# Head of a fused convolution and feed-forward kernel: dense conv of block 2 moved ahead of the second stage of block 0, a third of a weight copied by GpSimd, loads of x5 to x8 issued earlier, three matmuls on zeros fewer

## The chip, the cores and the metric

One core of one Trainium2 chip runs the whole program. The metric is the device time of one execution in microseconds (us). Eight executions of the kernel before have a median of 483.81 us, the lowest 480.97 and the highest 485.81.

## What is computed

```python
# x: (8, 4160, 192), weight: (8, 7), w1, w2, w3: (192, 768), w_out: (768, 192), all float32
w = softmax(weight, axis=-1)                  # one 7-tap filter for each of 8 heads
x_pad = zeros of 6 rows ahead of each sequence, then x
y[b, s, head h, :] = sum over k of w[h, k] * x_pad[b, s + k, head h, :]   # 24 channels a head
y = y.reshape(33280, 192)
h = max(max(y @ w1, y @ w2), y @ w3)
out = h @ w_out                               # (33280, 192) float32
```

## The kernel before, in words

**Blocks.** The 33280 tokens are cut into 65 blocks of 512. The maximum of three products is taken as a difference: with c = y w3, it is c + max(relu(y (w1 - w3)), y (w2 - w3)). So `make_wd` forms the two differences (tile wd, the upper 64 partitions for w1, the lower ones for w2), and the added c is folded into the second product through M = w3 w_out, which `make_m` computes once (tile m). For that, w3 is cast (`cast_w3`), transposed on TensorE (`transpose_w3`) and multiplied by w_out (tile wo). `copy_w3` copies w3 from partitions 0 to 63 to partitions 64 to 127 (tile w3s), in three parts of 256 columns, since the w2 half of `make_wd` needs it there: part 0 serves differences 0 and 1, part 1 serves 2 and 3, part 2 serves 4 and 5.

**Stages of a block t.** `load_x(t)` issues the DMA of its rows from SyncE's queue (SP). `cast_x(t)` casts them to float16 on GpSimd (POOL). `conv(t)` multiplies by a band matrix on TensorE (tile G), `evac` takes the result to SBUF (ys), `repack(t)` moves six pieces by DMA from the SP and POOL queues into the layout of the next product (yd), and `double(t)` copies yd to the other 64 partitions by DMA. Blocks 0 to 3 go another way, "dense": `cast_dense` writes two zero-padded copies (xz), `conv_dense` makes the convolution already in the right layout with 120 smaller matmuls (tile D), and the other half of yd comes from `cross` (three VectorE copies, blocks 0 and 1) or `cross_dma` (two DMAs on SP, blocks 2 and 3). Then `l1(t, j)`, for j of 0 to 5, makes 128 of the 768 hidden columns: three matmuls for lp and three for lq, interleaved, ScalarE's relu of lp (r, L376) and VectorE's maximum of r and lq (h, L377). `st2(t, u, 6)` is the second stage, in six parts: products of h by wo and of yd by m (po), ScalarE's copy a (L425), VectorE's sum o (L426). `store(t, ...)` writes the block.

**What sets the order.** Each engine works through its instructions in the order in which the kernel text issues them; the order is written by hand, and only waits on semaphores tie the engines. Lines 453 to 506 are the head: blocks 0 and 1, with the making of the weights woven in. From line 512 a loop over t = 2 to 64 issues l1(t, 0), two convolutions every second block, and then st2(t - 1, j) after each l1(t, j). `keep_warm(n)` (L213) issues n matmuls on a tile of zeros.

**Buffers that bind.** lp and lq have two PSUM buffers each, so l1 number k waits until r, or h, of number k - 2 is done. G, D, po and the zero matmuls share four others. Raw rows xf: blocks 0, 3 and 5 use one buffer, 1, 2 and 4 another, and from block 6 on there are four; so load_x(5) waits for cast_dense(3), and load_x(6) to load_x(9) wait for nothing. x16 (the cast rows) has four buffers.

**Lines to find.** The head's order is L453 to L506: cross(0) L459, make_wd(1, 2) L460, the zero matmuls L466, L468 and L474, copy_w3 part 2 on ScalarE L477, make_wd(4, 6) L479, cast_dense(2) L491, st2(0, 0) L492, conv_dense(2) L496, cross_dma(2) L497, load_x(5) and load_x(6) L500 and L501. In the loop, repack(4), load_x(7) and the casts of x5 and x6 are L531 to L534, and load_x(8) is L537.

Of the kernel before, what the change touches and what calls it, by code (L numbers as in the profile page):

```python
# [27 lines left out]
def kernel(  # L28
# [12 lines left out]
    nc = tc.nc  # L41
# [6 lines left out]
    NJ = DFF // P  # L48
# [105 lines left out]
    NC, NSLOT, CYC = D // HALF, D // 32, 96  # L154
# [54 lines left out]
    def keep_warm(n, pool=psw, tag="w"):  # L209

        ps = pool.tile([P, NBLK], FP32, tag=tag, name="idle")
        for _ in range(n):
            nc.tensor.matmul(ps[:], lhsT=idle[:, 0:P], rhs=idle[:], start=True, stop=True)  # L213
# [36 lines left out]
    def make_wd(j0, j1):  # L250
        f = slice(P * j0, P * j1)
        nc.vector.tensor_sub(out=wd[:, :, f], in0=ws[:, :, f], in1=w3s[:, :, f])  # L252

    def copy_w3(copy, part):
        f = slice(PW * part, PW * (part + 1))
        copy(out=w3s[HALF:P, :, f], in_=w3s[0:HALF, :, f])

    def cast_w3(part):
        f = slice(PW * part, PW * (part + 1))
        nc.gpsimd.tensor_copy(out=w3h[:, :, f], in_=w3s[0:HALF, :, f])  # L260

    def transpose_w3(g):
        ps = psw.tile([P, 2, D], FP32, tag="w", name=f"pt{g}")
        for k in range(2):
            js = slice(P * (2 * g + k), P * (2 * g + k + 1))
            for c in range(NC):
                nc.tensor.matmul(ps[:, k, HALF * c:HALF * (c + 1)], lhsT=w3h[:, c, js],
                                 rhs=ident16[0:HALF, 0:HALF], start=True, stop=True)
        nc.scalar.copy(out=w3t[:, 2 * g:2 * g + 2, :], in_=ps[:])
# [54 lines left out]
            else:  # L324
                copies[2](out=yd[0:HALF, 2, :], in_=ps[0:HALF, :])

    def cross(t):

        yd = dense[t]
        for c in range(NC):  # L330
            a, b = (slice(HALF, P), slice(0, HALF))[::-1 if c == 1 else 1]
            nc.vector.tensor_copy(out=yd[a, c, :], in_=yd[b, c, :])  # L332

    def cross_dma(t):
        yd = dense[t]
        nc.sync.dma_start(out=yd[HALF:P, 0:NC:2, :], in_=yd[0:HALF, 0:NC:2, :])
        nc.sync.dma_start(out=yd[0:HALF, 1, :], in_=yd[HALF:P, 1, :])
# [25 lines left out]
    def l1(t, j):  # L363


        N, y = blkN[t], dense[t]
        ps = [pool.tile([P, NBLK], FP32, tag=tag, name=f"l{tag}_{t}_{j}")
              for pool, tag in ((psp, "p"), (psq, "q"))]
        for c in range(NC):
            for i in range(2):  # L370
                row = slice(HALF * i, HALF * (i + 1))
                nc.tensor.matmul(ps[i][:, 0:N], lhsT=wd[row, c, P * j:P * (j + 1)],  # L372
                                 rhs=y[row, c, 0:N],
                                 start=(c == 0), stop=(c == NC - 1))
        r = rp.tile([P, NBLK], FP16, tag="r", name=f"r_{t}_{j}")
        nc.scalar.activation(out=r[:, 0:N], in_=ps[0][:, 0:N], func=AF.Relu)  # L376
        nc.vector.tensor_max(out=hs[t][:, j, 0:N], in0=r[:, 0:N], in1=ps[1][:, 0:N])  # L377

    def st2(t, u, NU):

        if t < 0:
            return
        hT, y = hs[t], dense[t]
        if u == 0:
            todo = [[], []]
            for s in range(4):
                tok = slice(P * s, P * (s + 1))
                for i in range(2):  # L390
                    row = slice(HALF * i, HALF * (i + 1))
                    mm = [(y[row, i, tok], m16[row, 0, :])]
                    if s % 2 == i:
                        mm.append((y[row, 2, tok], m16[row, 1, :]))
                    hh = [(hT[row, j, P * s:P * (s + 1)], wo[row, j, :]) for j in range(NJ)]
                    mm = hh + mm if t == 0 else mm + hh
                    todo[i] += [(s, n == 0, n == len(mm) - 1, m) for n, m in enumerate(mm)]
            if t == NB - 1:

                for i in range(2):  # L400
                    k = [sum(e[0] < s for e in todo[i]) for s in range(5)]
                    lot = [todo[i][k[s]:k[s + 1]] for s in range(4)]
                    todo[i] = lot[0][:-1] + lot[1][:-1] + lot[0][-1:] + lot[1][-1:] + lot[2] + lot[3]
            halves[t] = (todo, {})
        todo, ps = halves[t]
        n = len(todo[0])
        for e in range(n * u // NU, n * (u + 1) // NU):
            for i in range(2):
                s, first, last, (a, b) = todo[i][e]
                b0 = s if t == NB - 1 else s - s % 2  # L410
                if (b0, i) not in ps:
                    pool, tag = (psw, "w")
                    if t == NB - 1 and s in (1, 2):
                        pool, tag = (psp, "p") if i == 0 else (psq, "q")
                    ps[b0, i] = pool.tile([P, 2, D], FP32, tag=tag, name=f"po{i}_{t}_{s}")
                nc.tensor.matmul(ps[b0, i][:, s % 2, :], lhsT=a, rhs=b, start=first, stop=last)  # L416
            ends = {todo[i][e][0] for i in range(2) if todo[i][e][2]}
            for s in sorted(ends):
                done[t, s] = done.get((t, s), 0) + sum(todo[i][e][0] == s and todo[i][e][2] for i in range(2))
                if done[t, s] < 2 or (s % 2 == 0 and t < NB - 1):  # L420
                    continue
                s0 = s if t == NB - 1 else s - 1
                ss = slice(s0 % 2, s % 2 + 1)
                a = tp.tile([P, 2, D], FP32, tag="a", name=f"a_{t}_{s}")
                nc.scalar.copy(out=a[:, ss, :], in_=ps[s0, 0][:, ss, :])  # L425
                nc.vector.tensor_add(out=outs[t][:, s0:s + 1, :], in0=a[:, ss, :],  # L426
                                     in1=ps[s0, 1][:, ss, :])
                if t == NB - 1 and s % 2 == 1:
                    store(t, s - 1, s + 1, (nc.sync, nc.sync if s == 1 else nc.scalar))
# [26 lines left out]
    make_wd(0, 1)  # L456
    conv_dense(0, (nc.scalar.copy, nc.scalar.copy, nc.scalar.copy))
    keep_warm(4)
    cross(0)  # L459
    make_wd(1, 2)  # L460
    l1(0, 0)
    cast_dense(1, (nc.gpsimd.tensor_copy, nc.scalar.copy))
    cast_w3(0)
    copy_w3(nc.vector.tensor_copy, 1)
    l1(0, 1)
    keep_warm(1)  # L466
    conv_dense(1, (nc.scalar.copy, nc.scalar.copy, nc.scalar.copy))
    keep_warm(5)  # L468
    cross(1)
    make_wd(2, 3)  # L470
    l1(1, 0)
    make_wd(3, 4)
    cast_w3(1)
    keep_warm(1)  # L474
    l1(1, 1)
    transpose_w3(0)
    copy_w3(nc.scalar.copy, 2)  # L477
    l1(0, 2)
    make_wd(4, 6)  # L479
    cast_w3(2)  # L480
    keep_warm(1)
    l1(0, 3)
    transpose_w3(1)
    l1(1, 2)
    keep_warm(1)
    l1(1, 3)
    transpose_w3(2)
# [1 line left out]
    nc.gpsimd.tensor_copy(out=wo[:], in_=wos[:])  # L489
    l1(0, 5)  # L490
    cast_dense(2, (nc.gpsimd.tensor_copy, nc.gpsimd.tensor_copy))  # L491
    st2(0, 0, NJ)  # L492
    make_m(0)
    make_m(1)
    l1(1, 4)
    conv_dense(2, (nc.scalar.copy, nc.vector.tensor_copy, nc.scalar.copy))  # L496
    cross_dma(2)  # L497
    cast_dense(3, (nc.gpsimd.tensor_copy, nc.gpsimd.tensor_copy))
    cast_x(4)
    load_x(5)  # L500
    load_x(6)  # L501
    st2(0, 1, NJ)
    l1(1, 5)
    for u in range(2, NJ):
# [7 lines left out]
    for t in range(2, NB):  # L512
        if t > 3:
            load_x(t + 6)
            cast_x(t + 5)
        for u in doubles_at.get(t, (t + 2,)):
            double(u)
        begin(t)
        l1(t, 0)
        if t == 2:  # L520
            conv_dense(3, (nc.scalar.copy, nc.vector.tensor_copy, nc.scalar.copy))
            cross_dma(3)
        us = convs_at.get(t, (t + 3, t + 4) if t % 2 == 0 else ())
        for n, u in enumerate(us):
            conv(u, PQ if n or t == 2 else ((psw, "w"), (psw, "w")))
        for u in us:
            evac(u, 0)
        for u in us[::-1]:
            evac(u, 1, nc.vector.tensor_copy)
        if t == 2:  # L530
            repack(4)  # L531
            load_x(7)
            cast_x(5)
            cast_x(6)  # L534
        elif t == 3:
            repack(5)
            load_x(8)  # L537
            repack(6)
            load_x(9)
            cast_x(7)  # L540
            cast_x(8)
        else:
            repack(t + 3)
        st2(t - 1, 0, NJ)
        for j in range(1, NJ):
            l1(t, j)
            st2(t - 1, j, NJ)
            if t == NB - 1 and j == 3:
                store(t - 1, 0, 2, (nc.sync,))
        if t == NB - 1:  # L550
            store(t - 1, 2, 4, (nc.sync,))
        else:
            store(t - 1, 0, 4, (nc.gpsimd,))
# [30 lines left out]
```

## Time and profile before

| Quantity | Value |
|---|---|
| time of the profiled execution | 483.81 us |
| its span, from the first to the last instruction | 482.0 us (so 1.8 us lie around it) |
| median of 8 executions | 483.81 us (480.97 to 485.81) |
| TensorE (PE) busy | 472.3 us, 98% of the span |
| weight loads (PEld) busy | 390.1 us, 81% |
| VectorE (DVE) busy | 366.6 us, 76% |
| ScalarE (ACT) busy | 326.7 us, 68% |
| GpSimd (POOL) busy | 211.7 us, 44% |
| mean granted TensorE clock | 0.999 |
| 16 DMA engines, mean rate | 169 GB/s |

How to read the views of this profile: the page lists busy time by engine, a strip of 40 slices of the span, the DMA queues, the chain of work that ended last, and groups of instructions by source line with busy time, mean duration, and the idle time before them with what ended it. "L168 POOL CAST xz<-xf" is line 168, on GpSimd, a cast that writes xz and reads xf. The timeline gives start and duration of instructions in order of time, like ones merged, with the idle time of the engine before them in square brackets. The table by stretches gives each engine's busy time within a window of the span. PE busy counts overlapping matmuls, and their ends are modelled.

### The profile page before, as it was taken

Reading aid. Unit: us, or ns where it says so; the run is one execution under the profiler, and the core shown is the slowest. Engines: PE = TensorE matmul, PEld = TensorE weight load, DVE = VectorE, ACT = ScalarE, POOL = GpSimd, SP = SyncE. Lnnn points to the kernel's source line nnn. Section 1 sums busy time; section 2 is a strip of 40 time slices with the busy share of each in tenths; the row PEclk is TensorE's granted clock in tenths of the full one; section 3 lists DMA queues with packets and bytes.
Section 4 is the critical chain, followed back from the end, with each engine's and each line's share of the span. In section 5 each row is a group of like instructions: output and inputs, shape, how many; then the busy total and the mean of one; then the engine's idle time right before and its main releaser. Section 6 shows DMA issues by size and latency. Waiting matters only on the chain.

```text
span 482.0 us, 21861 instructions
## 1 busy us (share of the span) xinstructions
PE 472.3 (98%) x9045; PEld 390.1 (81%) x9045; DVE 366.6 (76%) x609; ACT 326.7 (68%) x611; POOL 211.7 (44%) x345
## 2 busy tenths in 40 slices
PE   8999899999999999999999999999999999999995
PEld 4367788888888888888888888888888888887995
DVE  4767678777877778777877777777877787777774
ACT  4656666676667667666767666766667666767663
POOL 4416345434534553454355435434543453455200
PEclk9999999999999999999999999999999999999999
DMA  8647776666676666747667676656766766664423
GB/s 199 169 102 204 207 197 176 172 174 175 177 185 180 171 180 165 203 141 186 188 169 194 159 195 179 179 161 166 195 178 175 202 165 172 179 171 102 110 73 99
DMA packets 68481, 81.68 MB, mean 169 GB/s; under 512 B 9342, under 2 KB 57486, under 8 KB 68382
## 3 DMA queue, kind: packets, MB, share of 16 engines
q1 hardware_dynamic: 55310, 49.41, 41.0%
q0 software_dynamic: 12912, 30.78, 21.0%
q8 instruction: 71, 1.16, 1.1%
q14 instruction: 28, 0.23, 0.2%
q10 hardware_dynamic: 160, 0.10, 0.1%
HBM read 30.31 MB, written 25.56 MB: 116 GB/s over the span
## 4 chain that ended last, share of the span: by engine, by line
PE 94%; DMA 1%; DVE 1%; ACT 1%; SPq 0%; issue 0%; POOL 0%; POOLq 0%; DVEq 0%
PE lp L372 30%; PE po L416 29%; PE lq L372 25%; PE G L297 6%; PE idle L213 2%; DMA xf<-in_x_dram 1%; PE D L316 1%; DMA yd<-yd 0%; ACT r L376 0%; DVE h L377 0%; DVE wd L252 0%; DVE yd L332 0%; SPq L355 0%; PE band_cols L235 0%; ACT yd L322 0%
## 5 line engine op out<-in xcount | busy, mean ns | idle before, releaser
L377 DVE TENSOR_TENSOR h<-r,lq 128x512 f16<-128x512 f16 x390 | 267.1, 685 | 100.9 <-ACT r L376 100.6
L376 ACT ACTIVATE r<-lp 128x512 f16<-128x512 f32 x390 | 232.8, 597 | 139.8 <-PE lp L372 91.6
L372 PE MATMUL lp<-yd,wd 64*128 64x512 f16 x1170 | 315.7, 376 | 0.8 <-ACT r L376 0.3
L372 PE MATMUL lq<-yd,wd 64*128 64x512 f16 x1170 | 315.0, 375 | 1.0 <-DVE h L377 0.9
L416 PE MATMUL po<-wo,h 64*128 64x192 f16 x3120 | 232.0, 243 | 0.0
L416 PEld LDWEIGHTS <-h 64*128 64x128 f16 x3120 | 186.4, 94 | 27.0 <-issue 0.2
L372 PEld LDWEIGHTS <-wd 64*128 64x128 f16 x2340 | 162.6, 93 | 26.5 <-issue 4.8
L442 POOL DMA_DIRECT2D out_dram<-o x63 | 50.8, 806 | 237.4 <-DVE o L426 222.5
L355 POOL DMA_DIRECT2D yd<-ys x183 | 92.3, 510 | 2.9 <-ACT ys L342 1.5
L416 PE MATMUL po<-m,yd 64*128 64x192 f16 x780 | 87.5, 243 | 0.0
L426 DVE TENSOR_TENSOR o<-a,po 128x384 f32<-128x384 f32 (+1 forms) x132 | 71.4, 541 | 1.0 <-ACT a L425 1.0
L425 ACT COPY a<-po 128x384 f32<-128x384 f32 (+1 forms) x132 | 61.7, 468 | 1.9 <-PE po L416 1.8
L149 POOL CAST x<-xf 112x960 f16<-112x960 f32 x60 | 59.7, 997 | 5.6 <-DMA xf<-in_x_dram 5.6
L416 PEld LDWEIGHTS <-yd 64*128 64x128 f16 x780 | 54.6, 94 | 8.4
L342 DVE CAST ys<-G 128x512 f16<-128x512 f32 x61 | 39.1, 681 | 1.6 <-PE G L297 1.6
L297 PEld LDWEIGHTS <-x 112*32 112x32 f16 x2400 | 28.6, 96 | 14.4 <-issue 12.7
L297 PE MATMUL G<-band,x 112*32 112x103 f16 (+1 forms) x2400 | 33.5, 209 | 1.6 <-POOL x L149 1.6
L342 ACT CAST ys<-G 128x512 f16<-128x512 f32 x61 | 33.0, 588 | 3.0 <-PE G L297 1.6
L213 PE MATMUL idle<-idle 128*128 128x512 f16 x27 | 10.3, 514 | 1.2 <-DVE idle L208 1.2
L213 PEld LDWEIGHTS <-idle 128*128 128x128 f16 x27 | 2.9, 119 | 6.7 <-issue 4.9
L168 POOL CAST xz<-xf 112x240 f16<-112x240 f32 (+2 forms) x15 | 4.8, 370 | 5.8 <-DMA xf<-in_x_dram 5.8
L316 PEld LDWEIGHTS <-xz 112*32 112x32 f16 x240 | 4.5, 107 | 1.9 <-issue 0.8
(48 smaller groups left out, 47.2 us busy)
## 6 DMA issues: line engine op xcount, KB each, us to landing
out_dram<-o POOLq DMA_DIRECT2D x63, 384.0 KB, 4.2
xf<-in_x_dram SPq DMA_DIRECT2D x57, 420.0 KB, 4.6
yd<-yd SPq DMA_DIRECT2D x61, 192.0 KB, 3.6
yd<-ys SPq DMA_DIRECT2D x61, 48.0 KB, 3.7
yd<-ys POOLq DMA_DIRECT2D x61, 48.0 KB, 3.3
xf<-in_x_dram SPq DMA_DIRECT2D x8, 252.0 KB, 4.3
yd<-ys POOLq DMA_DIRECT2D x61, 32.0 KB, 3.3
yd<-ys SPq DMA_DIRECT2D x61, 32.0 KB, 3.2
```

The costliest lines, as they stand in the source:

```text
L149: nc.gpsimd.tensor_copy(out=v[0:rl, q0:q1, :], in_=xf[0:rl, q0:q1, :])
L213: nc.tensor.matmul(ps[:], lhsT=idle[:, 0:P], rhs=idle[:], start=True, stop=True)
L297: nc.tensor.matmul(G[i][32 * g:32 * g + 32, lo:hi], lhsT=x16[0:rlen, cb:cb + 32], rhs=band[0:rlen, h, cc:cc + hi - lo], start=True, stop=T ...
L342: copy(out=slots[t][:, i, :], in_=convs[t][i][:])
L355: (nc.sync, nc.gpsimd)[n % 2].dma_start(out=yd[r0:r0 + rows, c, :], in_=slots[t][s0:s0 + rows, half, :])
L372: nc.tensor.matmul(ps[i][:, 0:N], lhsT=wd[row, c, P * j:P * (j + 1)], rhs=y[row, c, 0:N], start=(c == 0), stop=(c == NC - 1))
L376: nc.scalar.activation(out=r[:, 0:N], in_=ps[0][:, 0:N], func=AF.Relu)
L377: nc.vector.tensor_max(out=hs[t][:, j, 0:N], in0=r[:, 0:N], in1=ps[1][:, 0:N])
L416: nc.tensor.matmul(ps[b0, i][:, s % 2, :], lhsT=a, rhs=b, start=first, stop=last)
L425: nc.scalar.copy(out=a[:, ss, :], in_=ps[s0, 0][:, ss, :])
L426: nc.vector.tensor_add(out=outs[t][:, s0:s + 1, :], in0=a[:, ss, :], in1=ps[s0, 1][:, ss, :])
L442: qs[i].dma_start(out=bass.AP(tensor=out.tensor, offset=r * D, ap=[[D, n], [step * D, s1 - s0], [1, D]]), in_=ob[p0:p0 + n, s0:s1, :])
```

## The change

Nothing that is computed changes, only the place of some instructions, the engine of one copy, and the count of the matmuls on zeros. `cross` takes a list of the columns to be copied.

```diff
-    def cross(t):
+    def cross(t, cs=range(NC)):
         yd = dense[t]
-        for c in range(NC):
+        for c in cs:
...
     conv_dense(0, (nc.scalar.copy, nc.scalar.copy, nc.scalar.copy))
     keep_warm(4)
-    cross(0)
+    cross(0, (0,))
     make_wd(1, 2)
+    cross(0, (1, 2))
     l1(0, 0)
...
     l1(0, 1)
-    keep_warm(1)
     conv_dense(1, (nc.scalar.copy, nc.scalar.copy, nc.scalar.copy))
-    keep_warm(5)
+    keep_warm(4)
     cross(1)
     make_wd(2, 3)
     l1(1, 0)
     make_wd(3, 4)
     cast_w3(1)
-    keep_warm(1)
     l1(1, 1)
     transpose_w3(0)
-    copy_w3(nc.scalar.copy, 2)
+    copy_w3(nc.gpsimd.tensor_copy, 2)
     l1(0, 2)
-    make_wd(4, 6)
     cast_w3(2)
     keep_warm(1)
     l1(0, 3)
+    make_wd(4, 5)
     transpose_w3(1)
     l1(1, 2)
+    make_wd(5, 6)
     keep_warm(1)
     l1(1, 3)
...
     cast_dense(2, (nc.gpsimd.tensor_copy, nc.gpsimd.tensor_copy))
-    st2(0, 0, NJ)
+    conv_dense(2, (nc.scalar.copy, nc.vector.tensor_copy, nc.scalar.copy))
+    cast_dense(3, (nc.gpsimd.tensor_copy, nc.gpsimd.tensor_copy))
+    cast_x(4)
+    load_x(5)
+    cross_dma(2)
+    load_x(6)
+    load_x(7)
     make_m(0)
     make_m(1)
     l1(1, 4)
-    conv_dense(2, (nc.scalar.copy, nc.vector.tensor_copy, nc.scalar.copy))
-    cross_dma(2)
-    cast_dense(3, (nc.gpsimd.tensor_copy, nc.gpsimd.tensor_copy))
-    cast_x(4)
-    load_x(5)
-    load_x(6)
+    st2(0, 0, NJ)
     st2(0, 1, NJ)
     l1(1, 5)
...
         if t == 2:
             repack(4)
-            load_x(7)
+            load_x(8)
             cast_x(5)
             cast_x(6)
         elif t == 3:
             repack(5)
-            load_x(8)
             repack(6)
             load_x(9)
```

## The prediction

> **What bounds the kernel now.** I read the table by stretches first, to see where TensorE is not full.
>
> ```profile
> core 0: us, PE busy (x) PEld busy (x) DVE busy (x) ACT busy (x) POOL busy (x), PEclk, DMA share, GB/s
> ...
> 10.00:20.00 10.00, 9.56 (x123) 4.04 (x119) 7.85 (x14) 7.08 (x15) 3.74 (x5) 1.00 0.95 215
> 20.00:30.00 10.00, 8.76 (x148) 4.93 (x145) 6.54 (x11) 5.82 (x12) 4.96 (x13) 1.00 0.16 46
> ...
> 50.00:60.00 10.00, 8.54 (x164) 7.25 (x166) 6.75 (x11) 5.75 (x11) 4.56 (x7) 1.00 0.86 232
> 60.00:70.00 10.00, 10.00 (x215) 8.23 (x212) 7.82 (x13) 7.22 (x14) 6.11 (x10) 1.00 0.72 197
> ```
>
> From 52 us on PE has no gap until the last block: the loop is bound by matmuls, so what the head saves or loses reaches the end one for one. PE's holes lie ahead of 52 us, and all of the change does too. I then took the holes from TensorE's timeline. The largest is at 49.8 us:
>
> ```profile
> 49.26 0.64 PE L297 MATMUL G<-band,x 112*32 112x103 f16 x40
> 51.46 0.32 PE L297 MATMUL G<-band,x 112*32 112x103 f16 x12 [1.56 <-POOL x L149]
> ```
>
> ```profile
> 50.41 0.99 POOL L149 CAST x<-xf 112x960 f16<-112x960 f32 x1 [2.27 <-DMA xf<-in_x_dram]
> ```
>
> conv(8) waits for the cast of x8, and that for its load, issued by SP only at 45.06 us. The second is at 32.09, where l1(2, 0) has its first matmul but waits for cross_dma(2), issued at 30.13. The third kind is the chain of waits between 17 and 26 us:
>
> ```profile
> 17.03 0.61 ACT r L376
> 17.66 0.69 DVE h L377
> 18.35 0.48 DVE wd L252
> 18.83 0.34 ACT w3t L269
> 19.31 0.83 ACT w3s L256
> 20.17 0.61 ACT r L376
> ...
> 21.40 1.00 DVE wd L252
> 22.48 0.69 DVE h L377
> ```
>
> Here the two engines behind TensorE set the pace, and a 0.83 us copy on ScalarE and a double-width difference on VectorE (listed at 1.15) stand in it.
>
> Last, VectorE between 10 and 13 us, beside GpSimd:
>
> ```profile
> 10.21 2.03 DVE L332 COPY yd<-yd 64x512 f16<-64x512 f16 x3 [2.13 <-ACT yd L322]
> 12.27 0.56 DVE L252 TENSOR_TENSOR wd<-ws,w3s 128x384 f16<-128x384 f32 x1
> ```
>
> ```profile
> 10.13 1.65 POOL L260 CAST w3h<-w3s 64x768 f16<-64x768 f32 x2
> ```
>
> The copy's median is 0.29 us, yet the first two take 0.89 (10.21) and 0.80 (11.13), each ending 0.15 after one of GpSimd's casts.
>
> **What the Trainium skill says.** "SBUF — State Buffer", Who interferes with whom: VectorE and GpSimd share a port pair under an exclusive lock; a copy in a two-port mode, or a VectorE operation with two SBUF inputs against a GpSimd operation that reads SBUF, blocks fully. The trace agrees both ways: the copies above; the double-width difference at 21.40; and the GpSimd cast that met it, in this row, at 1.11 where the median is 0.32:
>
> ```profile
> L168 POOL CAST xz<-xf x12: 253/322/1114, 20.1 to 23.7; 112x240 f16<-112x240 f32 x4, 112x160 f16<-112x160 f32 x4, 112x80 f16<-112x80 f32 x4
> ```
>
> "TensorE: Matmul & The Clock Gate", What's actually happening: the array falls to half rate after about 3.4 us of idleness. The trace shows a slow start (8 zero matmuls in 3.59 us at 4.97, 0.45 each, against 5 in 1.25 at 14.99) and no later fall.
>
> **The change part by part.**
>
> *Three zero matmuls fewer.* Some 0.25 us each, 0.75 busy. But L466's ends at about 13.9, and conv_dense(1) behind it needs ScalarE's cast_dense(1), done at 13.85; the fifth at L468 ends at 16.2, when the crossing of column 1 ends too; the one at L474 precedes l1(1, 1), after which l1(0, 2) waits for h(1, 0) until 18.35. All three fill waits: I count 0 (bounds 0 and 0.75 gain).
>
> *make_wd(1, 2) between the crossing copies.* VectorE does the same work to 12.83 in either order: copies, then difference, before; copy, difference, two copies, after. The difference would start at 11.13, meet GpSimd's second cast (to 11.78), end near 12.22, and the two copies at 12.54 and 12.83 instead of 11.93 and 12.24. So l1(0, 0) ends its lp 0.6 later, r(0, 0) starts at 13.2 instead of 12.60, and behind it on ScalarE cast_dense(1) ends at 14.46 instead of 13.85. conv_dense(1) is late by 0.54; l1(1, 0) had 0.1 of slack in its order, so r(1, 0) starts at 17.46 instead of 17.03: a loss of 0.43. Bounds: 0, if the difference isn't blocked and hides beside the cast; 0.6.
>
> *The weight third on GpSimd.* Nearest row: L260, the same elements in, 0.82 us. "GPSIMD Engine Reference", Elementwise, gives 1.03 cycles an element where the port binds and about 1.8 for a tight loop: 768 elements at 1.2 GHz are 0.66 to 1.15, an estimate; the trace of before doesn't show the copy. I take 0.82. It lies at 13.0 to 13.8, cast_w3(2) behind it to 14.65; GpSimd is free until wo at 18.77, so its own time costs nothing. VectorE's copy_w3(1) then runs into cast_w3(2) by 0.15, or 0.5 at the upper price; the crossing of block 1 waits for ScalarE until 15.9 anyhow: 0, at most 0.2. Who needs part 2 is make_wd(4, 5), after 22. Without that cover the copy would cost its 0.82.
>
> *ScalarE freed and make_wd(4, 6) split.* In l1 one link from h(k - 2) to h(k) is 0.04 to the matmul, 0.61 to the end of lp, 0.03, r 0.60, 0.03, h 0.69: 2.0 us, as h(0, 3) at 23.17 to h(1, 3) at 25.17 shows. Two such chains alternate. With r(1, 0) at 17.46: h(1, 0) ends at 18.78, the difference (3, 4) at 19.3, h(1, 1) at 20.0; h(0, 2), without the ScalarE copy, at 20.83 (before 21.49); h(0, 3), without the wide difference before it, at 22.04 (23.17); the difference (4, 5), met by a cast, to 22.65; h(1, 2) at 23.34 (23.75); (5, 6) to 23.95; h(1, 3) at 24.6 (25.17). l1(0, 5) then ends at 25.25 instead of 25.87. From r(1, 0) on 1.05 is won, less the 0.43: net 0.6.
> One point is tight: the difference (3, 4) reaches VectorE at 18.70, and wo's cast (1.14) starts on GpSimd when wos lands, 18.77. If the cast is first, the difference is blocked until 19.9 and ends at 20.3; followed through, l1(0, 5) ends some 0.3 later than before.
>
> *conv_dense(2) ahead.* The work on TensorE is the same: conv_dense 1.03, make_m 1.25, two l1 0.65 each, st2 2.6. cast_dense(2) ends near 22.1, so it doesn't wait. VectorE's evacuation of D now stands ahead of m, which l1(1, 4) waits for: 0.1 to 0.15. ScalarE's evacuations end at about 27.1, and SP issues cross_dma(2) then, not at 30.13; with up to 4.2 us to landing (as for block 3's) that is 31.3, before l1(2, 0) is reached at about 31.65. l1(2, 0) started at 32.09 and its matmuls ended 0.65 later than unbroken (32.57 and 32.95 for 32.09 and 32.30). Gain 0.65 - 0.15 = 0.5; bounds 0 and 0.65.
>
> *Loads.* Moved past cross_dma(2): one issue of load_x(5), which waits for cast_dense(3), done at 24.07, so no wait for the crossing at 27; it may still have rows in flight to 29, included above. Behind the crossing come load_x(6) and load_x(7), 0.55 each on SP, done by 30, ahead of the crossing of block 3 (due near 34). load_x(8), two issues, 1.07 us, moves ahead of double(4) in place of load_x(7): that queue stood idle from 39.74 to 40.82, so 0.5 more still fits. On SP it leaves the stretch ahead of repack(6), which is then earlier. x8 lands before 45; GpSimd casts it right after x7 (47.15 to 48.15), by 49.1, ahead of conv(8) at 49.8. The 1.56 hole goes; next late would be that cast, with 0.7 of slack. Bounds 1.0 and 1.56.
>
> *Sum.* 0.6 + 0.5 + 1.56 = 2.66. The profiled execution took 483.81 (span 482.0 and 1.8 around it), which is also the median: 483.81 - 2.66 = 481.15, given as 481.2.
>
> **The rivals.** (1) wo's cast wins the lock: -0.3 for 0.6, with the rest: 1.76, 482.05, say 482.1. For it: 0.07 us decides. Against: in the trace of before VectorE is first. (2) No slip at 10 to 13 us: the difference isn't blocked, or the casts come later. Then 0.43 more, 480.7. Against: the 1.11 cast. (3) The loads don't help: x5 to x7 in flight hold the moves back, and conv(8) waits elsewhere (repack on GpSimd late, so the cast of x8 too). Without the 1.56, 482.7, within the bound. That the moved load does not move cannot be: the order of the built program has it between repack(4) and double(4). (4) Slower: the clock. The head now has waits on TensorE at 11.7 to 12.5, 13.8 to 14.5 and 16.5 to 16.8, with three zero matmuls fewer. If the array falls to half rate in one window around 15, l1 matmuls take 0.43 for 0.215, each link gains 0.4 to 0.6, and dense work doubles. One window of 3.4 costs up to 3.4, two 6.8; above 2.66 the change loses. Two windows, less the gains: 483.81 - 2.66 + 6.8 = 487.9. Against: no hole reaches 0.9 us.
>
> **How the numbers follow.** Forecast 0.47, (1) 0.24, (2) 0.14, (3) 0.09, (4) 0.06. What a measurement of this kernel can tell from no change is about 0.3%, 1.45 us, so faster is below 482.36. Of the forecast 0.44 lie there, of (1) 0.17, of (2) 0.13: 0.74. Within: 0.03 + 0.07 + 0.01 + 0.08 = 0.19. Slower: 0.01 + 0.06 = 0.07. The range takes in (2) with the zero matmuls at their full 0.75 (479.95) and (3) (482.7), each with 0.5 more for measurement: 479.5 to 483.2, which leaves out (4) and the edges.
>
> **What would show it.** The hole ahead of conv(8) gone and the cast of x8 directly behind x7's; r(1, 0) near 17.5; h(0, 5)'s predecessor l1(0, 5) ending at 25.25; a wo cast of 1.14 and a difference (3, 4) of 0.55 (in rival 1, 1.6); l1(2, 0) unbroken. Wrong if zero matmuls late in the head show 0.45 us each, or if a new hole stands before conv(5), l1(3, 0) or l1(5, 0).

## The result, and the profile after

The changed kernel takes 480.17 us (median of 11 executions, 478.98 to 480.79), the kernel before 483.69 us (median of 32 in the same comparison): a difference of the medians of 3.5 us. The ratio is 0.9922 (0.78% faster), with a 95% interval of 0.9908 to 0.9937. The forecast was 481.2 us from 483.81, a gain of 2.6, so 0.9 us of the gain was not foreseen. The profiled execution of the changed kernel took 479.85 us, with a span of 478.0 us.

I put marks into both traces that stand in the same order in both kernels, and read how much earlier each is reached. The last column is the forecast's working for the same stretch. The end of l1(0, 5) is taken as the start of its last matmul plus 0.22 us, the distance to a next one.

| Mark (us from the start of the span) | before | after | gained on the way to it | forecast |
|---|---|---|---|---|
| r(1, 0) starts | 17.03 | 16.93 | 0.10 | -0.43 |
| l1(0, 5) ends | 25.87 | 24.65 | 1.12 | 1.05 |
| conv_dense(3) starts | 33.49 | 31.70 | 0.57 | 0.5 |
| conv(7) starts | 49.26 | 47.33 | 0.14 | 0 |
| the next pair of convolutions starts | 64.95 | 61.28 | 1.74 | 1.56 |
| last instruction | 482.0 | 478.0 | 0.33 | 0 |
| sum | | | 4.00 | 2.7 |

All but the last 0.33 us are gained in the head and the first steps of the loop, and the signs of all but the first are those of the forecast. The last 0.33 are not spread over the loop. Some 0.19 of them come at one place, where ten matmuls of st2 took 0.85 us in before (at 123.90) and 0.58 in the changed kernel (at 120.23), and 0.10 come around 443 us of before. It is not the clock: from 60 us on the granted clock is 1.00 in both traces until the last 2 us of the span, in which TensorE has no work. What held before up at these two places stays open.

The table by stretches of the changed kernel, for three of the windows shown of before:

```profile
core 0: us, PE busy (x) PEld busy (x) DVE busy (x) ACT busy (x) POOL busy (x), PEclk, DMA share, GB/s
10.00:20.00 10.00, 9.31 (x121) 4.05 (x118) 8.32 (x15) 7.00 (x15) 5.90 (x8) 1.00 1.04 225
20.00:30.00 10.00, 9.45 (x167) 5.90 (x166) 6.80 (x12) 5.79 (x12) 4.88 (x13) 1.00 0.45 117
50.00:60.00 10.00, 10.00 (x152) 8.88 (x148) 7.50 (x13) 6.71 (x13) 5.69 (x9) 1.00 0.91 231
```

PE has 0.69 us more work in the window from 20 to 30 us (9.45 for 8.76) and 1.46 more from 50 to 60 (10.00 for 8.54). From 10 to 20 it is less busy than before (9.31 for 9.56): there the zero matmuls are missing, and the work is not much earlier. The clock is full in all of them.

TensorE's timeline, then GpSimd's, at conv(7) and conv(8):

```profile
47.33 1.10 PE L297 MATMUL G<-band,x 112*32 112x103 f16 x80
```

```profile
45.35 1.92 POOL L149 CAST x<-xf 112x960 f16<-112x960 f32 x2
```

The 80 matmuls of the two convolutions run in one piece, since x8 is cast directly behind x7 (x2 in one line) and is ready at 47.27. The hole of 1.56 us is gone.

The chain of waits between 17 and 26 us in the changed kernel:

```profile
17.56 0.70 DVE h L377
...
18.30 0.37 PE lq L372
...
21.45 0.77 DVE wd L252
22.23 0.22 DVE h L377
...
22.75 0.60 DVE wd L252
23.35 0.61 DVE h L377
```

No ScalarE copy is left in it, and the wide difference of 1.00 us has become two, of 0.77 and 0.60, with an h between them.

VectorE and GpSimd between 10 and 16 us:

```profile
10.21 0.48 DVE L332 COPY yd<-yd 64x512 f16<-64x512 f16 x1 [1.87 <-ACT yd L322]
10.73 0.56 DVE L252 TENSOR_TENSOR wd<-ws,w3s 128x384 f16<-128x384 f32 x1
11.32 1.12 DVE L332 COPY yd<-yd 64x512 f16<-64x512 f16 x2
12.97 0.69 DVE L377 TENSOR_TENSOR h<-r,lq 128x512 f16<-128x512 f16 x1 [0.53 <-ACT r L376]
13.69 1.20 DVE L256 COPY w3s<-w3s 64x768 f32<-64x768 f32 x1
```

```profile
10.17 1.23 POOL L168 CAST xz<-xf 112x240 f16<-112x240 f32 x3 [6.47 <-DMA xf<-in_x_dram]
11.35 1.77 POOL L260 CAST w3h<-w3s 64x768 f16<-64x768 f32 x2
13.52 0.82 POOL L256 COPY w3s<-w3s 64x768 f32<-64x768 f32 x1 [0.40 <-DMA w3s<-in_moe_w_dram]
```

Two things are to be seen. The difference (1, 2) took 0.56, so it was not blocked; the casts of x1, which started only at 10.17, were (1.23 for three, 0.85 before). And VectorE's copy of a weight third at 13.69, which took 0.69 in the first trace of before, took 1.20: it started while GpSimd's new copy ran.

Then l1(2, 0), three of its six matmuls:

```profile
30.95 0.38 PE L372 MATMUL lp<-yd,wd 64*128 64x512 f16 x1
...
31.16 0.38 PE L372 MATMUL lp<-yd,wd 64*128 64x512 f16 x1
...
31.38 0.38 PE L372 MATMUL lp<-yd,wd 64*128 64x512 f16 x1
```

They stand 0.21 and 0.22 apart: the wait for cross_dma(2) is gone.

### The profile page after: what moved, and what is told of

It reads as the page before. It is cut to its first block, busy times and chain, and to the rows that moved or that the text cites. A ratio compares the mean times of both kernels' runs of the same rounds, so it can differ in the third digit from the quotient of the medians.

```text
span 478.0 us, 21859 instructions
## 1 busy us (share of the span) xinstructions
PE 470.4 (98%) x9042; PEld 392.0 (82%) x9042; DVE 366.2 (77%) x610; ACT 325.6 (68%) x610; POOL 213.1 (45%) x346
## 3 DMA queue, kind: packets, MB, share of 16 engines
q8 instruction: 71, 1.16, 1.1%
## 4 chain that ended last, share of the span: by engine, by line
PE 96%; DVE 2%; ACT 0%; issue 0%; DVEq 0%
PE lp L372 32%; PE po L416 30%; PE lq L372 26%; PE G L297 7%; PE idle L213 1%; DVE h L377 1%; PE D L316 1%; DVE wd L252 0%; DVE yd L332 0%; DVE w3s L256 0%; ACT yd L322 0%; PE band_cols L235 0%; DVE yd L323 0%; DVE m L282 0%; DVE o L426 0%
## 5 line engine op out<-in xcount | busy, mean ns | idle before, releaser
L213 PE MATMUL idle<-idle 128*128 128x512 f16 x24 | 9.2, 527 | 1.2 <-DVE idle L208 1.2
```

## The experiments

After the result my theory was: the forecast holds, except that the moved difference (1, 2) isn't blocked, because the order in which VectorE and GpSimd reach the lock was other than in the trace of before. The rivals were that the extra microsecond comes from somewhere else: the zero matmuls (forecast at 0), the crossing of block 2, or the loads. With 6 executions a ratio has an interval of about 0.2 to 0.3% to either side, 1.0 to 1.5 us; effects of half a microsecond are therefore read from the marks in the profile, and the times only bound them. The marks move between executions too, by 0.2 to 0.4 us where the last pair of runs lets one see it. All edits are made to the changed kernel, unless another is named, and none leaves out any of the computation.

**The load of x8 late again.**

```diff
-            load_x(8)
             cast_x(5)
...
             repack(5)
+            load_x(8)
             repack(6)
```

> The changed kernel with load_x(8) put back to its old place at t = 3, between repack(5) and repack(6); x5 to x7 stay early. Theory 1 (the hole ahead of conv(8) is only the late issue of x8): the hole of 1.56 to 1.7 us is back between the two convolutions of t = 4, GpSimd's cast of x8 waits some 2 us for its rows, and the kernel takes 1.6 to 1.8 us more than the changed kernel: 481.8 to 482.0. Rival (the queue that is emptier by x7 alone mends it): no hole, 480.2.

Measured: 481.82 us (17 executions), ratio to before 0.9962 (0.9944 to 0.9979). TensorE's timeline and GpSimd's cast of x8:

```profile
47.07 0.64 PE L297 MATMUL G<-band,x 112*32 112x103 f16 x40
49.25 0.64 PE L297 MATMUL G<-band,x 112*32 112x103 f16 x40 [1.54 <-POOL x L149]
```

```profile
48.21 0.99 POOL L149 CAST x<-xf 112x960 f16<-112x960 f32 x1 [2.11 <-DMA xf<-in_x_dram]
```

The hole is back with 1.54 us and the next pair of convolutions starts at 62.74 instead of 61.28. By the times 1.65 us come from this one moved load, nearly half of the gain, as the forecast had it.

**conv_dense(2) back behind st2(0, 0), make_m and l1(1, 4).**

```diff
+    st2(0, 0, NJ)
+    make_m(0)
+    make_m(1)
+    l1(1, 4)
     conv_dense(2, (nc.scalar.copy, nc.vector.tensor_copy, nc.scalar.copy))
...
     load_x(7)
-    make_m(0)
-    make_m(1)
-    l1(1, 4)
-    st2(0, 0, NJ)
     st2(0, 1, NJ)
```

> The changed kernel with st2(0, 0), make_m and l1(1, 4) put back ahead of conv_dense(2), the loads still ahead of moves. Theory 1 (what conv_dense(2) ahead wins is the wait of l1(2, 0) for cross_dma(2), nothing else): l1(2, 0) is broken again by about 0.65 us, perhaps more since x5's rows are now in flight; 0.5 to 0.8 us more than the changed kernel, 480.7 to 481.0. Rival (the crossing by DMA lands in time anyway since the head is 1.1 us earlier): no gap, 480.2.

Measured: 480.43 us, ratio 0.9927 (0.9899 to 0.9955), 0.26 us above the changed kernel, so nothing that the times can tell. In its trace SP issues cross_dma(2) at 28.42 instead of 26.52, and l1(2, 0) is broken:

```profile
30.38 0.38 PE L372 MATMUL lp<-yd,wd 64*128 64x512 f16 x1
30.87 0.37 PE L372 MATMUL lq<-yd,wd 64*128 64x512 f16 x1
31.21 0.37 PE L372 MATMUL lp<-yd,wd 64*128 64x512 f16 x1
```

The second lp matmul comes 0.83 after the first, for 0.21 in the changed kernel: 0.6 us are lost there. From the end of l1(0, 5), at 24.17 here and at 24.65 in the changed kernel, to conv_dense(3), at 31.75 and 31.70, are 7.58 and 7.05 us: 0.53 lost, where the forecast has 0.5 (before needs 7.62). The trace bears the step out in place and size; the times alone would not have shown it.

**The crossing of block 0 whole, then the difference, as before.**

```diff
-    cross(0, (0,))
+    cross(0)
     make_wd(1, 2)
-    cross(0, (1, 2))
```

> The changed kernel with cross(0) whole again and make_wd(1, 2) after it. Theory 1 (the forecast: the difference between the copies is blocked by GpSimd's casts and holds the crossing back by 0.6 us): this kernel is 0.3 to 0.5 us faster than the changed one, 479.7 to 479.9, if the rows of block 1 land near 9.3 us. Rival (they land later, the difference is not blocked and hides in VectorE's wait for ScalarE): this kernel is slower by 0.1 to 0.5 us, 480.3 to 480.7.

Measured: 479.7 us (477.97 to 481.86), ratio 0.9908 (0.9877 to 0.994). The median lies where the forecast's theory had it (479.7 to 479.9), but six executions that spread over 3.9 us do not tell a gain of 0.4 from a loss of 0.4. The trace does not settle the swap either, because the profiled execution began otherwise. TensorE's timeline of this kernel, then of the changed one:

```profile
4.92 1.90 PE L213 MATMUL idle<-idle 128*128 128x512 f16 x8
6.98 1.09 PE L316 MATMUL D<-band,xz 112*32 112x103 f16 x60 [0.16 <-ACT band L239]
```

```profile
4.97 3.59 PE L213 MATMUL idle<-idle 128*128 128x512 f16 x8
8.49 0.79 PE L316 MATMUL D<-band,xz 112*32 112x103 f16 x26
```

The same eight zero matmuls took 1.90 us instead of 3.59, so conv_dense(0) started 1.5 us earlier. VectorE was through with the three copies by 9.80, before the casts of x1 began at 10.31; the difference ended at 10.38, and nothing met. Part of the lead was lost again: cross_dma(2) was issued at 23.86, behind load_x(5), and l1(2, 0) waited for it (0.52 and 0.19 us). The swap needed another experiment.

**The weight third's copy back on ScalarE, make_wd(4, 6) whole again.**

```diff
-    copy_w3(nc.gpsimd.tensor_copy, 2)
+    copy_w3(nc.scalar.copy, 2)
     l1(0, 2)
+    make_wd(4, 6)
...
-    make_wd(4, 5)
...
-    make_wd(5, 6)
```

> The changed kernel with copy_w3 part 2 back on ScalarE and make_wd(4, 6) as one operation back after l1(0, 2). Theory 1 (the chain of h sets the pace from 17 to 26 us, copy and wide difference stand in it): from the start of r(1, 0) to the end of l1(0, 5) 8.8 us instead of 7.7; 1.0 to 1.2 us more than the changed kernel, 481.2 to 481.4. Rival (the won time is from conv_dense(1) starting earlier, and the chain has slack): less than 0.4 us more, below 480.6.

Measured: 479.86 us, ratio 0.9917 (0.9892 to 0.9942): not slower, against what I expected. The trace shows a part of it. Its chain of waits has the wide difference back:

```profile
20.65 1.00 DVE wd L252
21.65 0.67 DVE h L377
```

From r(1, 0), at 16.79, to the end of l1(0, 5), near 25.03, are 8.24 us: 0.52 more than in the changed kernel (7.72), where I had looked for 1.05, and 0.60 less than before (8.84). (Three other variants that leave this stretch alone, with the load of x8 late, conv_dense(2) back and the doublings first, take 7.43 to 7.65, so 0.52 is the low end of what the edit costs.) So the step as a whole gains the 1.1 that was forecast, but not by this edit alone; what before has besides is the three zero matmuls. conv_dense(3) is 0.58 later than in the changed kernel (32.28), and the profiled execution took 0.42 longer (480.27). The other five took 479.54 to 480.57, so their median shows nothing: half a microsecond is below what six executions tell.

**The three zero matmuls back.**

```diff
     l1(0, 1)
+    keep_warm(1)
     conv_dense(1, (nc.scalar.copy, nc.scalar.copy, nc.scalar.copy))
-    keep_warm(4)
+    keep_warm(5)
...
     cast_w3(1)
+    keep_warm(1)
     l1(1, 1)
```

> The changed kernel with its three zero matmuls put back (one ahead of conv_dense(1), the fifth behind it, one ahead of l1(1, 1)). Theory 1 (as forecast: all three fill waits): no change, 480.2, and the same distance from r(1, 0) to the end of l1(0, 5), 7.7 us. Rival (the one ahead of l1(1, 1) stands in a chain: l1(1, 1), the transpose, ScalarE's copy of it, r(0, 2)): r(1, 1) starts 0.3 later against r(1, 0), l1(0, 5) ends 0.2 to 0.5 later, 480.4 to 480.7.

Measured: 480.43 us, ratio 0.9928 (0.991 to 0.9946). conv_dense(1) starts at 13.87, 0.43 later, but r(1, 0) at 16.93 and conv_dense(2) at 24.66, conv_dense(3) at 31.62: at every later mark within 0.1 of the changed kernel. The forecast's 0 is not contradicted, but not pinned down either: in this execution ScalarE's first evacuation of block 0 came 0.23 us earlier (9.37 for 9.60), so up to 0.23 may have been lost on the way to r(1, 0), and the median is 0.26 above the changed kernel's, which six executions do not tell from 0. The run also completes the one before: r(0, 2) starts 2.01 us behind r(1, 0) in the changed kernel, 2.15 with the zero matmuls back, 2.62 with ScalarE's copy back, and 3.14 with both, as before. The zero matmul ahead of l1(1, 1) costs 0.14 alone and 0.52 with ScalarE's copy behind it. VectorE shows why conv_dense(1)'s 0.43 is lost by r(1, 0). This is its crossing of block 1:

```profile
15.26 0.29 DVE L332 COPY yd<-yd 64x512 f16<-64x512 f16 x1
15.80 0.29 DVE L332 COPY yd<-yd 64x512 f16<-64x512 f16 x1 [0.26 <-ACT yd L323]
```

Here the copies wait for ScalarE's evacuation. In the changed kernel ScalarE is earlier, but VectorE is later (15.64, then 0.93 without a break for the three copies), since its copy of a weight third took 1.20 there and 0.71 here.

**GpSimd's casts of weights moved away from the crossing of block 0.** cast_w3(0) goes ahead, before the convolution of block 0; cast_w3(1) and (2) go behind a later step, and the cast of wo moves forward by two steps.

```diff
     copy_w3(nc.vector.tensor_copy, 0)
+    cast_w3(0)
     make_wd(0, 1)
...
     cast_dense(1, (nc.gpsimd.tensor_copy, nc.scalar.copy))
-    cast_w3(0)
     copy_w3(nc.vector.tensor_copy, 1)
...
     make_wd(3, 4)
-    cast_w3(1)
     l1(1, 1)
...
     copy_w3(nc.gpsimd.tensor_copy, 2)
+    cast_w3(1)
     l1(0, 2)
-    cast_w3(2)
...
     l1(1, 3)
+    nc.gpsimd.tensor_copy(out=wo[:], in_=wos[:])
+    cast_w3(2)
     transpose_w3(2)
     l1(0, 4)
-    nc.gpsimd.tensor_copy(out=wo[:], in_=wos[:])
     l1(0, 5)
```

> The changed kernel with GpSimd's casts of w3 kept out of the crossing of block 0: part 0 cast ahead of cast_dense(1), part 1 behind the copy of part 2, part 2 behind wo. Theory 1 (the lock between VectorE's copies and GpSimd's casts holds l1(0, 0) back, by how much depends on when the rows of block 1 land, 9.3 to 10.6 us so far): the crossing's copies take 0.29 each but for what meets cast_dense(1), conv_dense(1) starts at 12.7 to 13.0 instead of 13.2 to 13.75, and l1(0, 5) ends 0.4 to 0.8 earlier than in the changed kernel; 479.5 to 479.8. Rival (VectorE's copies are slow for another reason, the half-filled lanes or ScalarE's writes to the same tile): they still take 0.5 to 0.9.

Measured: 480.62 us, ratio 0.994 (0.9923 to 0.9957). VectorE's timeline:

```profile
10.67 0.56 DVE L252 TENSOR_TENSOR wd<-ws,w3s 128x384 f16<-128x384 f32 x1
11.26 0.61 DVE L332 COPY yd<-yd 64x512 f16<-64x512 f16 x2
...
15.02 1.33 DVE L332 COPY yd<-yd 64x512 f16<-64x512 f16 x3
```

Without a cast beside them the two copies take 0.61 instead of 1.12, and conv_dense(1) starts at 12.88 instead of 13.44: the long copies are the neighbour's doing, not the copies' own. But the moved casts meet the crossing of block 1 (1.33 for three copies), r(1, 0) is only 0.22 earlier, and conv_dense(2) not at all (24.80 for 24.73).

**Four zero matmuls for eight ahead of conv_dense(0).** This asks whether the start that varies is worth shortening.

```diff
-    keep_warm(8, psp, "p")
+    keep_warm(4, psp, "p")
```

> The changed kernel with 4 zero matmuls instead of 8 ahead of conv_dense(0). Theory 1 (the eight, at half clock, 0.45 us each, are what conv_dense(0) waits for; in the run with the whole crossing they ran at full clock and the head was 1.5 us ahead): conv_dense(0) starts at 6.8 to 7.0 instead of 8.49, and the head gains 1.0 to 1.5 us: 478.7 to 479.2. Rival (the clock rises only after enough work): the matmuls behind run at half clock for longer and eat it: 480 or more.

Measured: 479.79 us (478.65 to 480.92), ratio 0.9918 (0.9898 to 0.9938). TensorE's timeline:

```profile
4.91 1.04 PE L213 MATMUL idle<-idle 128*128 128x512 f16 x4
6.70 1.09 PE L316 MATMUL D<-band,xz 112*32 112x103 f16 x60 [0.76 <-ACT band L239]
```

In this execution conv_dense(0) starts at 6.70 (8.49 in the changed kernel) and conv_dense(3) at 30.28 (31.70), and it took 478.7. But most of that is not the edit: the four matmuls took 0.26 us each, the rate of the fast start in the run with the whole crossing (eight in 1.90, 0.24 each), not the 0.45 of the changed kernel. Against that run, which kept all eight, conv_dense(0) is only 0.28 earlier. What four matmuls save in an execution that starts slowly, no trace shows. Others of the same kernel took up to 480.9, so the gain is not shown.

**No zero matmuls behind conv_dense(0).** All ten that are left there go, which tries the forecast's slower rival.

```diff
-    keep_warm(4)
     cross(0, (0,))
...
-    keep_warm(4)
     cross(1)
...
-    keep_warm(1)
     l1(0, 3)
...
-    keep_warm(1)
     l1(1, 3)
```

> The changed kernel with none of the zero matmuls behind conv_dense(0) (10 fewer). Theory 1 (they fill waits; no wait in the head is long enough for the clock to fall): l1 matmuls stay 0.21 us apart, the time is within 0.4 us of the changed kernel, 479.8 to 480.3. Rival, the forecast's slower case (the clock falls): l1 matmuls 0.43 us apart for 3.4 us or more, 482 to 487.

Measured: 480.52 us (479.21 to 481.67), ratio 0.9933 (0.9913 to 0.9953); the profiled execution took 481.67, the longest. Its table by stretches, with the granted clock third from the end:

```profile
14.00:16.00 2.00, 0.94 (x27) 0.59 (x17) 1.91 (x4) 1.74 (x3) 1.63 (x2) 1.00 1.07 273
16.00:18.00 2.00, 2.00 (x12) 0.97 (x11) 1.46 (x4) 0.60 (x1) 0.00 (x0) 0.65 1.13 233
18.00:20.00 2.00, 2.00 (x15) 0.71 (x13) 2.00 (x3) 1.17 (x3) 1.43 (x2) 0.50 0.61 149
```

The clock falls to half from about 16.6 to 20.0 us, and l1 matmuls come 0.42 apart instead of 0.21. In the changed kernel it is 1.00 in all three windows, with PE busy 1.91 of the 2.00 us from 14 to 16; here PE is busy 0.94 of them, and 2.26 of the 3.40 us from 13.20 to 16.60 (3.31 in the changed kernel), with no wait above 0.79 us. The Trainium skill, "TensorE: Matmul & The Clock Gate", What's actually happening, ties the fall to an idle window of about 3.4 us; here short waits in a stretch two thirds full were enough, and the measurement decides. conv_dense(1) had started at 12.79, 0.65 ahead of the changed kernel, and conv_dense(2) starts at 25.21, 0.48 behind it: 1.1 us are lost on the way. Not all of that need be the clock's. In the same stretch GpSimd's cast of wo reached the lock ahead of VectorE's difference (3, 4):

```profile
18.09 1.14 POOL L485 CAST wo<-wos 128x1152 f16<-128x1152 f32 x1 [2.39 <-DMA wos<-in_moe_w_out_dram]
```

```profile
18.15 1.49 DVE L252 TENSOR_TENSOR wd<-ws,w3s 128x384 f16<-128x384 f32 x1
```

The difference took 1.49 instead of 0.55, and the h behind it, which l1(0, 3) waits for, came late with it. So the rival's mechanism is real, and the window's price here is at most 1.1; how the 1.1 splits between clock and lock is not shown. (This execution took 1.8 us more than the changed kernel's profiled one; besides the 0.48 at conv_dense(2), 0.87 are one wait for a doubling at 55.8 us.)

**Doublings of blocks 5 and 6 ahead of the loads of x9 and x10.** In the changed kernel the 192 KB moves of these two blocks landed 6.2 and 5.9 us after their issue behind the loads, and I suspected that the spread between executions came from them.

```diff
-        if t > 3:
+        if t > 4:
             load_x(t + 6)
             cast_x(t + 5)
...
             double(u)
+        if t == 4:
+            load_x(9)
+            load_x(10)
+            cast_x(9)
...
             repack(6)
-            load_x(9)
```

> The changed kernel with the loads of x9 and x10 behind the doubling moves of blocks 5 and 6 in SP's queue, not ahead of them. Theory 1 (in the changed kernel the doubling of block 5 lands 6.2 us after its issue, behind x9 and x10, about 0.5 us ahead of l1(5, 0), so some executions wait there): it lands within 4.5 us of its issue, no execution waits, the profile's span is as in the changed kernel to 0.3 us, and the times lie closer together, 479.6 to 480.2 in the median. Rival (x9 is now late, or the spread comes from elsewhere): same or wider spread, or a wait of the cast of x9 that reaches TensorE, 480.5 or more.

Measured: 479.88 us (477.87 to 481.66), ratio 0.9921 (0.989 to 0.9952). The two moves land after 2.6 and 5.0 us, and the time doesn't follow; the spread is no smaller. That theory fell. The fastest execution had a mean granted clock of 1.000, the two slowest 0.996 and 0.997; but one of 479.48 us had 0.997 as well, so where the spread comes from stays open.

**Four for eight, doublings first, and cross_dma(2) ahead of load_x(5).** The version that the runs pointed to: the edits of the two kernels called four for eight and doublings, and

```diff
-    load_x(5)
     cross_dma(2)
+    load_x(5)
```

> Four zero matmuls for eight ahead of conv_dense(0), the doubling moves ahead of x9 and x10, and cross_dma(2) ahead of load_x(5). Theory 1 (the four save 1.4 us of head, and what took it back in half of the executions of the run with four was the doubling move of block 5): 478.3 to 479.0, all executions within 1 us. Rival (the clock's phase decides, so half of the executions keep a slow stretch): 479.5 to 480.2, in two groups.

Measured: 478.85 us (478.14 to 480.22), ratio 0.9898 (0.9874 to 0.9921), the lowest median of all. TensorE's timeline:

```profile
4.93 1.04 PE L213 MATMUL idle<-idle 128*128 128x512 f16 x4
6.86 1.09 PE L316 MATMUL D<-band,xz 112*32 112x103 f16 x60 [0.89 <-ACT band L239]
```

conv_dense(0) waits for ScalarE's table instead of for zeros; conv_dense(3) is at 29.68, 2.0 us earlier than in the changed kernel, and l1(2, 0) is unbroken although it starts at 28.93. But this trace has the fast start too (0.26 us for each of the four), and the profiled execution of the run with the whole crossing, which has that start and none of these edits, took 478.15, as long as this one (478.14). The spread is 2.1 us, where I had looked for 1. The two intervals overlap, so "better than the changed kernel by about 1.3 us" is not shown, nor which of the three edits would bring it.

**The kernel before once more, and the swap alone.** Before unchanged, for a second trace of its head, and before with nothing but the swap:

```diff
-    cross(0)
+    cross(0, (0,))
     make_wd(1, 2)
+    cross(0, (1, 2))
```

> The kernel before, once more, for the landing of the rows of block 1 (9.34 us in its first profile). Theory 1 (that landing varies by execution, and the forecast was made on an early one): another landing between 9.3 and 10.7; if it is above 10, the crossing's copies of block 0 are blocked less or not at all and conv_dense(1) starts before 13.8 instead of at 13.96. Rival (it is the order of the kernel's loads that sets it): 9.34 again within 0.1.

> The kernel before with make_wd(1, 2) between the copies of cross(0), nothing else. Theory 1 (forecast): with the rows of block 1 landing below 9.6 us the crossing's last copies end 0.5 to 0.6 later and conv_dense(1) starts near 14.5, 484.2; landing above 10, no loss, conv_dense(1) at about 13.96 behind its zero matmul, 483.8. Rival (the swap hides the difference and gains): conv_dense(1) before 13.7 and 483.3.

Measured: 483.14 us for before (its one execution); 482.64 us (22 executions) for the swap, ratio to before 0.9982 (0.9966 to 0.9999), a gain of about 0.9 us (0.05 to 1.6) where the forecast had a loss of 0.43. The casts of x1 began at 9.83 in the second trace of before (9.34 in the first) and at 9.61 with the swap, so the landing differs between executions of one kernel. VectorE's timeline in the second trace of before, and then with the swap:

```profile
9.84 0.89 DVE L332 COPY yd<-yd 64x512 f16<-64x512 f16 x2 [1.33 <-ACT yd L322]
11.05 0.71 DVE L332 COPY yd<-yd 64x512 f16<-64x512 f16 x1 [0.32 <-ACT yd L325]
11.79 1.06 DVE L252 TENSOR_TENSOR wd<-ws,w3s 128x384 f16<-128x384 f32 x1
...
13.48 1.15 DVE L256 COPY w3s<-w3s 64x768 f32<-64x768 f32 x1
```

```profile
9.93 0.28 DVE L332 COPY yd<-yd 64x512 f16<-64x512 f16 x1 [1.49 <-ACT yd L322]
10.25 0.56 DVE L252 TENSOR_TENSOR wd<-ws,w3s 128x384 f16<-128x384 f32 x1
10.84 1.12 DVE L332 COPY yd<-yd 64x512 f16<-64x512 f16 x2
...
13.21 1.16 DVE L256 COPY w3s<-w3s 64x768 f32<-64x768 f32 x1
```

In the old order it is here the difference that meets a cast (1.06); in the new one the difference passes, and the second of the two copies, which only lq waits for, bears the wait. (The copies of a weight third, 1.15 and 1.16 here, met a cast of weights on GpSimd, from 13.27 and from 13.00.) On TensorE, the first matmul of l1(0, 1) in the second trace of before, and with the swap:

```profile
12.91 0.39 PE L372 MATMUL lp<-yd,wd 64*128 64x512 f16 x1 [0.72 <-DVE wd L252]
```

```profile
12.02 0.39 PE L372 MATMUL lp<-yd,wd 64*128 64x512 f16 x1
```

In before l1(0, 1) waits for the difference (in its first trace too, at 12.89, after 0.22 idle); with the swap it follows l1(0, 0) without a break. Counted from ScalarE's first evacuation of block 0, which differs by up to 0.37 us between executions that start alike, r(1, 0) comes after 7.43 and 7.82 us in the two traces of before and after 7.09 with the swap alone, 0.3 and 0.7 earlier. That is one trace against two which differ by 0.39 themselves; in the changed kernel the distance is 7.33, and 7.56 with its zero matmuls back. So the traces show that the loss did not come; the size of the gain rests on the times. And it is no gain in every execution: in the run with the whole crossing, where the start was early and nothing met, the distance is 6.82.

## Why the forecast was right, and where it failed

The three steps that were to carry the gain were right in mechanism and in size, each seen by its own run. The forecast was 1.0 us too slow, in part because one step had the wrong sign.

*Loads.* Right, mechanism and place. The hole was 1.56, the first experiment put 1.54 of it back, and the mark gained 1.74; the remaining 0.2 around it is not explained.

*conv_dense(2) ahead.* Right: 0.57 for 0.5. The 0.65 of the broken l1(2, 0) came back, and about half of the 0.15 was lost that I took off for VectorE's evacuation of D.

*ScalarE freed and make_wd(4, 6) split.* Right in sum, 1.12 for 1.05. (From r(1, 0) to the end of l1(0, 5) the three traces with before's order of this stretch take 8.61 to 8.84, and the changed kernel with the three variants named above 7.43 to 7.72, so the step is worth 0.9 to 1.4.) The reason was incomplete: putting the copy and the wide difference back costs 0.52, putting the zero matmuls back costs nothing in this stretch, and both together, as in before, 1.12. So part of the gain belongs to two edits at once. The tight point, wo's cast against the difference (3, 4), fell as forecast: the difference ran from 18.16 and took 0.55, the cast from 18.49 took 1.22. The first rival did not occur in this trace, but that is in part luck of the landing: in the second trace of before the cast was first, at 18.18, and the difference from 18.29 took 1.45, and the same is seen without the zero matmuls behind conv_dense(0).

*Three zero matmuls fewer.* Within its bounds; 0 and a gain of 0.2 are not told apart. With ScalarE's copy in the chain, as in before, the one ahead of l1(1, 1) was not free: it cost 0.52.

*make_wd(1, 2) between the crossing copies.* This step failed: a loss of 0.43 was forecast, and by the times the swap alone gains about 0.9 (0.05 to 1.6). In all eleven traces with the swap the difference took 0.56 to 0.62. The working had the difference reach the lock at 11.13, second to a cast that ends at 11.78. That copied the order of arrival from the trace of before, where the first cast of weights came at 10.13, 0.08 ahead of VectorE's copy at 10.21. But those casts stand behind the casts of x1, and x1 landed to be cast from 9.34 in that trace, 0.26 ahead of ScalarE's first evacuation of block 0, and from 9.50 to 10.64 in the thirteen others, 0.12 or more behind it. With x1 later VectorE's difference comes first, and GpSimd waits; in two of the traces GpSimd's first cast of weights began only 0.03 behind it. What the swap does in an execution where x1 lands as early as in the first trace of before, no run shows. The Trainium skill, "SBUF — State Buffer", Who interferes with whom, has the rule in a sentence that I should have used: "Issue order, not op shape, decides who blocks." I used the lock and took the order for given. The second error in the step: I let conv_dense(1) hang on ScalarE's cast_dense(1) alone, when l1(0, 1), just ahead of it, was waiting for the very difference that the swap brings forward. The idle time of 0.22 in front of it was in the trace. My second rival, no slip at 10 to 13 us, is what happened; its 480.7 us still had no gain from the swap in it.

*The weight third on GpSimd.* The copy took 0.82, as taken from the row of casts. Its own time cost nothing, as forecast. VectorE's copy at 13.69 met it and took 1.20, and the crossing of block 1 began at 15.64. The meeting is not the new copy's doing alone: in the second trace of before, and with the swap alone, VectorE's copy met the old cast in that place and took 1.15 and 1.16. What differs is the cover. I had put the meeting at 0 to 0.2, because the crossing would wait for ScalarE until 15.9 anyhow. ScalarE's second evacuation ended at 15.42, since conv_dense(1) had become earlier, by 0.52. So of these 0.52 only 0.10 reached r(1, 0). In the second trace of before the copy's 1.15 was hidden, since the crossing there still waited for ScalarE until 15.92. The cover of one step was taken away by another step of the same change.

*The slower rival.* Its mechanism was seen when all ten zero matmuls were left out, and its sum was too high. At half clock TensorE falls behind by half of a stretch, so the 3.4 us from 16.6 to 20.0 can cost at most 1.7, not 3.4, and two such stretches 3.4, not 6.8. With the three zero matmuls of this change left out, the clock stayed at 1.00.

The gain left over is then: 0.53 from the first mark (0.10 for -0.43), 0.07 in l1, 0.07 at conv_dense(3), 0.14 ahead of conv(7), where one short stall of before is missing, 0.18 at the loads, and 0.33 behind 61 us; 1.32 in all between the two profiled executions, of which the medians show 0.9.

## What to carry to other kernels

Where two engines share a lock, don't carry the order of arrival from one trace into the forecast: find what releases each of them, and if one hangs on a DMA that lands within the other's slack, work the case out both ways. Then look at which of the delayed operations has someone waiting for it: the order to choose is the one in which the blocked operation has slack. And work out covers after the change, not before it: a wait that hides a cost may be what another part of the same change removes.

## What the runs showed of the hardware that I had not expected

- A load in flight is enough to turn a lock over. In the two traces of the kernel before, the cast of x1 began, when its load had landed, at 9.34 and 9.83 us; in the first the crossing's copies were held (0.89 and 0.80, for 0.29 alone) and the difference (1, 2) took 0.56, in the second it took 1.06. Two casts of weights on GpSimd took 1.59 to 2.05 over all traces.
- The eight zero matmuls at the start took 3.59 us in eleven traces and 1.90 in another, where only instructions after them differ. A start that looks fixed in one profile isn't, and an edit of the start must be compared with an execution that started alike.
- The granted clock fell to half for 3.4 us after 3.4 us in which TensorE was busy 2.26 us, with no wait above 0.79 us. In the six executions of that kernel its mean was 0.994 to 0.999.
